# Start of a fused attention, rational and PReLU kernel: two load queues, shared key blocks, a wide exponential, more idle products, paired chunks

## The chip, the cores and the metric

The kernel runs on one core of a Trainium2 chip. The metric is device time in microseconds (us), the median of several runs. The engines are TensorE (PE; its weight loads are PEld), VectorE (DVE), ScalarE (ACT), GpSimd (POOL, unused here) and SyncE (SP), which issues the transfers.

## The reference

Attention over 4 batches, 8 heads, 576 positions, head width 64, each query seeing 32 keys; then two MLPs over 2304 tokens (512 to 2048 to 512):

```python
mask_plain = (rel >= 0) & (rel < window)                                             # heads 0-3
mask_dil = (rel >= 0) & (rel < window * dilation) & (rel % dilation == 0)            # heads 4-7
attn = softmax(where(mask, scale * q @ k.T, -1e9)); x = attn @ v
h = x @ w_in;  P = a0 + a1*h + a2*h**2 + a3*h**3;  Q = 1 + |b0|*|h| + |b1|*h**2
x = (P / (Q + 1e-6)) @ w_out                    # first MLP
h = x @ w_in2; out = (max(h, 0) + alpha * min(h, 0)) @ w_out2   # second MLP
```

The weights come as 64-bit words.

## The kernel before

The 2304 tokens are cut into five blocks (256, 512, 512, 512, 512). Attention is cut into 18 units of 256 queries and four heads, plain or dilated; block 0 has units 0 (plain) and 1 (dilated), block 1 units 2 to 5, and so on. A unit is eight cells: 32 queries against 64 keys, for four heads on four groups of partitions. Its steps:

- `qk_load`, `v_load` (L430, L442): transfers by SP. Each cell brings its 64 keys, so the 32 keys that two neighbouring cells share come twice.
- `att_s` (L456): on PE, the mask is added into two PSUM banks by products of an identity with a mask (L471, bf16), then 32 score products (L482, f32; the trace counts two matmuls and two weight loads for each).
- `att_max`, `att_exp` (L491, L502): DVE takes each row's maximum; ACT computes eight exponentials, 64 columns each, with the maximum as bias and the sum as by-product (L513).
- `att_den`, `att_norm`/`att_norm2`, `att_t` (L518 to L541): one over the sum, the scaling (on DVE for units 0 and 1, on ACT later, L528), the transpose on DVE.
- `att_pv` (L543): products with the values (L557); `att_hi`, `att_lo` (L587): copies into the x tiles.

A first-MLP step takes a chunk of 128 hidden features: `inproj` (L613) multiplies the block's x by a chunk of `w_in` into a bank `ps_h` (two buffers); `rat_1`, `rat_2` (L640, L648) compute the rational function on ACT and DVE; `outproj1` (L668) adds the chunk's share of the output into four banks `ps_y`. Chunks go in pairs J. Block 0 runs in plain f32, one product where later blocks take three. `w_convert` (L383) turns a pair of raw 64-bit chunks into f32: two passes on ACT (L395), three on DVE (L398, L400). `w_split` (L409) makes the two parts for blocks 1 to 4. The second MLP works on the stored result of the first.

A planner, `in_order_of_need` (L155), fixes the order of PE, DVE, ACT and SP up to its own 197 us (`ORDERED`): with costs from `_cost` (L122) it takes, on the engine that can start first, the ready instruction with the longest path behind it. Idle products (bf16, 128x512, of a zeroed tile `warm`) come last: PE gets them where nothing else is ready in the plan. There are 8 at the start (`WARM`, L961) and 20 more (`FILLS`, L965). The order of the first loads is a string: c the mask table, a a unit's queries, keys and values, p the coefficients, w a weight chunk. The planner also models instruction supply on PE: it counts words per product, and a block of 256 may not be opened sooner than 6.5 us after the last.

```python
ORDER = "capawwwwawwwwwwwwww"
words = 4 if todo[k].ins[0].dtype == F32 else 2
if (fetched + words) // FETCH > fetched // FETCH:
    start = max(start, opened + FETCH_NS)
```

Of the kernel before, what the change touches and what calls it, by code (L numbers as in the profile page):

```python
# [31 lines left out]
FILLS = (20,)  # L32
W_BIAS = 2.0 ** -112
# [13 lines left out]
KW = UB // 2 * HEADS * CELL  # L47
# [5 lines left out]
ORDER = "capawwwwawwwwwwwwww"  # L53


class Unit:


    def __init__(self, block, dilated, part):
# [6 lines left out]
        self.vw = self.segs * (self.nb + 1) * D  # L66

# [82 lines left out]

def _is_filler(i):
    return i.engine == mybir.EngineType.PE and i.ins[0].dtype == BF16 and _columns(i.outs[0]) == FILL


def in_order_of_need(tc, nc, places, late):  # L155
# [18 lines left out]
    for k, i in enumerate(todo):  # L174
# [7 lines left out]
        if i.engine == Engine.SP:  # L182
            size[k] = writes[0][2] - writes[0][1], (writes[0][4] - writes[0][3])
# [48 lines left out]
    for k in reversed(range(n)):  # L232
        own = costs[k][1] if todo[k].engine != Engine.SP else 2500 + size[k][0] * size[k][1] / 400
# [9 lines left out]
    free = {Engine.PE: 1300.0, Engine.DVE: 800.0, Engine.Activation: 1500.0, Engine.SP: 730.0}  # L243
# [6 lines left out]
    fetched, opened = 63, 0.0  # L250
    for _ in range(n):
        pick = None
        for e, w in waiting.items():
            if not w:
# [6 lines left out]
        k = max((k for k in waiting[e] if ready_at[k] <= limit), key=lambda k: level[k])  # L261
# [12 lines left out]
        if e == Engine.SP:  # L274
# [22 lines left out]
def attn_rational_prelu_kernel(  # L297
# [9 lines left out]
    alpha: bass.AP,  # L307
# [18 lines left out]

    def bank(tag, bufs=1):
# [10 lines left out]
    co = cp.tile([128, 6], F32, name="co")  # L338
# [4 lines left out]
    alp = cp.tile([128, NC], F32, name="alp")  # L343
# [112 lines left out]
    def att_s(U, tags=("aS", "aP"), banks=None):  # L456
# [3 lines left out]
        kinds = [[UNITS[U].mask(2 * jj + p) for jj in range(HALF)] for p in range(2)]  # L460
# [30 lines left out]
    def att_max(U):  # L491
        a = att[U]
        mx = sp.tile([128, 8], F32, tag="mx", name="mx", bufs=2)
        nm = a["nm"] = sp.tile([128, 8], F32, tag="nm", name="nm", bufs=2)
        for p in range(2):
# [107 lines left out]
    h_t, tmp, g_t, acc = {}, {}, {}, {}  # L603

# [8 lines left out]
    def inproj(item):  # L613
# [3 lines left out]
        hp = bank("h", 2)[:, :BLOCKS[n]]  # L617
# [335 lines left out]

    nc.scalar.preload_act_table_set("natural_log_exp_and_others")
# [244 lines left out]
```

## Time and profile before

| | us |
|---|---|
| median of three runs | 866.67 (866.16 to 866.96) |
| profiled execution | 867.52 |
| its span, first to last instruction | 865.7 |
| PE busy | 843.1 (97%) |
| DVE busy | 722.8 (83%) |
| ACT busy | 560.2 (65%) |

The span is that of the profiled execution; the other 1.8 us of it lie outside. A busy PE counts products at either clock, so the granted clock has to be read beside it.

### The profile page before, as it was taken

To read this page: it belongs to the slowest core of one execution; us is meant where nothing else is said; L and a number is where in the kernel's file an instruction comes from. 1 tells how busy PE (TensorE), PEld (TensorE's weight loads), DVE (VectorE), ACT (ScalarE), POOL (GpSimd) and SP (SyncE) were. 2 spreads that over 40 slices of the span, in tenths; PEclk is the share of its full clock that TensorE was granted. 3 is DMA by queue.
4 is the path that set the end of the run, shared out by engine and by line. 5 is a ranking of instruction groups with operands and counts; after the bars stand their busy time and mean duration, and the time that the engine had idled before them with its cause. 6 is when DMAs were issued, how large, how long until landed. Compare 5 with 4: busy or idle time off the path is not lost.

```text
span 865.7 us, 15595 instructions
## 1 busy us (share of the span) xinstructions
PE 843.1 (97%) x6258; PEld 717.7 (83%) x6260; DVE 722.8 (83%) x1066; ACT 560.2 (65%) x1092; POOL 0.2 (0%) x4
## 2 busy tenths in 40 slices
PE   7888999999999989999999999999999999999998
PEld 4677878888888777788888898988989899899896
DVE  4799999989889878899899899999976769767652
ACT  4799986777866786665757566557553546635424
POOL 0000000000000000000000000000000000000000
PEclk8899999999999999999999999999999999999999
DMA  9892211133632355320202333315120102300001
GB/s 354 307 405 79 81 50 36 53 101 135 236 104 103 120 181 187 108 88 15 76 25 83 125 122 121 98 61 175 70 80 24 49 30 75 122 26 25 0 1 73
DMA packets 33912, 90.93 MB, mean 105 GB/s; under 512 B 4016, under 2 KB 11568, under 8 KB 33840
## 3 DMA queue, kind: packets, MB, share of 16 engines
q1 hardware_dynamic: 33840, 89.94, 29.6%
q8 instruction: 49, 0.80, 0.4%
q14 instruction: 23, 0.19, 0.1%
HBM read 74.72 MB, written 15.20 MB: 104 GB/s over the span
## 4 chain that ended last, share of the span: by engine, by line
PE 74%; DVE 11%; ACT 11%; issue 2%; DMA 1%; SPq 0%; ACTq 0%
PE ps_h L838 20%; PE ps_y L696 15%; PE ps_h L624 14%; PE ps_y L676 13%; PE ps_aS L696 4%; PE ps_aP L696 4%; ACT p L513 3%; ACT p L528 2%; DVE tc L656 2%; DVE tb L652 1%; DVE tc L646 1%; ACT ta L643 1%; DVE tc L657 1%; DVE tc L645 1%; ACT tc L644 1%
## 5 line engine op out<-in xcount | busy, mean ns | idle before, releaser
L624 PE MATMUL ps_h<-xh,winh 128*128 128x512 f32 x256 | 102.8, 401 | 3.9 <-DVE tc L646 3.8
L624 PE MATMUL ps_h<-xl,winh 128*128 128x512 f32 x256 | 100.6, 393 | 1.1 <-DVE xl L594 1.1
L624 PE MATMUL ps_h<-xh,winl 128*128 128x512 f32 x256 | 100.3, 392 | 0.0
L676 PE MATMUL ps_y<-gh,wouth 128*128 128x512 f32 x256 | 99.2, 390 | 0.6 <-ACT gh L665 0.6
L676 PE MATMUL ps_y<-gl,wouth 128*128 128x512 f32 x256 | 99.7, 389 | 0.0
L676 PE MATMUL ps_y<-gh,woutl 128*128 128x512 f32 x256 | 99.7, 389 | 0.0
L643 ACT ACTIVATE ta<-ps_h,root 128x512 f32<-128x512 f32 (+1 forms) x80 | 52.7, 659 | 51.1 <-DVE tc L656 32.4
L696 PE MATMUL ps_y<-wouth,gl 128*128 128x512 f32 x192 | 75.0, 391 | 0.0
L696 PE MATMUL ps_y<-woutl,gh 128*128 128x512 f32 x192 | 74.9, 390 | 0.0
L696 PE MATMUL ps_y<-wouth,gh 128*128 128x512 f32 x192 | 74.3, 390 | 0.0
L843 ACT ACTIVATE n<-h 128x768 f32<-128x768 f32 x48 | 40.5, 843 | 42.8 <-DVE h L868 23.3
L624 PEld LDWEIGHTS ps_h<-xh,winh 128*128 128x128 f32 x256 | 48.4, 189 | 17.2 <-DVE tc L646 6.1
L645 DVE TENSOR_TENSOR tc<-tc,ps_h 128x512 f32<-128x512 f32 (+1 forms) x80 | 50.1, 627 | 12.8 <-ACT tc L644 12.7
L845 DVE SCALAR_TENSOR_TENSOR n<-n,alp,h 128x768 f32<-128x768 f32 x48 | 48.8, 1016 | 13.7 <-ACT h L844 13.0
L644 ACT ACTIVATE tc<-ps_h,co 128x512 f32<-128x512 f32 (+1 forms) x80 | 60.1, 751 | 0.0
L624 PEld LDWEIGHTS ps_h<-xl,winh 128*128 128x128 f32 x256 | 48.5, 190 | 11.3 <-DVE xl L594 1.8
L676 PEld LDWEIGHTS ps_y<-gh,wouth 128*128 128x128 f32 x256 | 48.1, 188 | 10.8 <-ACT gh L665 1.0
L624 PEld LDWEIGHTS ps_h<-xh,winl 128*128 128x128 f32 x256 | 48.4, 189 | 10.3
L734 ACT ACTIVATE st_a<-w 128x1024 fp32r<-128x1024 f32 x24 | 25.4, 1057 | 48.3 <-PE ps_h L838 45.2
L653 ACT ACTIVATE ta<-tb,c1t 128x1024 f32<-128x1024 f32 (+1 forms) x40 | 43.2, 1080 | 20.5 <-DVE tb L652 20.4
L676 PEld LDWEIGHTS ps_y<-gh,woutl 128*128 128x128 f32 x256 | 48.0, 188 | 9.9
L676 PEld LDWEIGHTS ps_y<-gl,wouth 128*128 128x128 f32 x256 | 48.0, 188 | 9.9
(187 smaller groups left out, 2168.9 us busy)
## 6 DMA issues: line engine op xcount, KB each, us to landing
ld_qk<-in_qk_dram SPq DMA_DIRECT2D x16, 768.0 KB, 5.3
w<-w_dram_in SPq DMA_DIRECT2D x24, 512.0 KB, 3.2
raw<-in_w_in_dram SPq DMA_DIRECT2D x16, 512.0 KB, 4.9
raw_inh<-in_w_out_dram SPq DMA_DIRECT2D x13, 512.0 KB, 7.3
out_dram<-os SPq DMA_DIRECT2D x18, 256.0 KB, 2.1
raw_inh<-in_w_in_dram SPq DMA_DIRECT2D x8, 512.0 KB, 8.5
raw_outh<-in_w_in_dram SPq DMA_DIRECT2D x8, 512.0 KB, 9.2
raw_outh<-in_w_out_dram SPq DMA_DIRECT2D x8, 512.0 KB, 9.3
```

The costliest lines, as they stand in the source:

```text
L513: nc.scalar.activation(out=a["p"][:, j * CELL:(j + 1) * CELL], in_=a["s"][p][:, jj * CELL:(jj + 1) * CELL], func=AF.Exp, scale=scale, bias ...
L624: product = nc.tensor.matmul(out=hp, lhsT=w, rhs=x, start=(k == 0), stop=(k == len(pairs) - 1))
L643: nc.scalar.activation(out=ta, in_=hp, func=AF.Abs, scale=root)
L644: nc.scalar.activation(out=tc_, in_=hp, func=AF.Identity, scale=co[:, 3:4], bias=co[:, 2:3])
L645: nc.vector.tensor_tensor(out=tc_, in0=tc_, in1=hp, op=ALU.mult)
L653: nc.scalar.activation(out=ta, in_=tb, func=AF.Ln, bias=c1t)
L676: nc.tensor.matmul(out=yt, lhsT=w[:, m * 128:(m + 1) * 128], rhs=g, start=(c == 0 and i == 0), stop=(c == NC - 1 and i == len(pairs) - 1),)
L696: nc.tensor.matmul(out=yt, lhsT=g[:, tok], rhs=w, start=(first and i == 0), stop=(last and i == 2))
L734: nc.scalar.activation(out=hi, in_=t, func=AF.Copy)
L838: nc.tensor.matmul(out=hp, lhsT=u[:, ws], rhs=x[:, xs], start=(k == 0), stop=(k == 5))
L843: nc.scalar.activation(out=neg, in_=h, func=AF.Relu, scale=-1.0)
L845: nc.vector.scalar_tensor_tensor(out=neg, in0=neg, scalar=alp[:, c:c + 1], in1=h, op0=ALU.mult, op1=ALU.subtract, reverse1=True)
```

## The change

- **Loads.** The mask table goes over ACT's queue. SP begins with unit 0's queries and keys, as one transfer into the single `ld_qk` buffer, then unit 1's, then unit 0's values and two weight chunks. `coef` and `alpha` are one transfer.
- **Keys.** A run of neighbouring cells shares its keys: 5 blocks of 32 keys for four cells in a row, 6 for two rows of two, in place of 8 (`run`, `kb`, `kw`, `block_of`). The first four cells go to one bank, the last four to the other, where it was even and odd.
- **Unit 0's exponential.** DVE adds the negated maximum to the scores (two passes, 256 columns each), ACT takes one exponential of 512 columns, DVE sums (one pass).
- **Idle products.** 40 in place of 20 after the first 8, in groups of two; the second of a group, and all mask products of a unit but the first, are written with `ldweights=False` (`held`). The planner keeps a group together and counts one word for such a product.
- **Block 0's pairs.** The two chunks of a pair lie in one bank, and `rat_1` works on both at once, 512 columns.
- The planner treats ACT's transfer as a transfer (`_is_dma`).

```diff
-KW = UB // 2 * HEADS * CELL
+KW = 6 * HEADS * QB
-ORDER = "capawwwwawwwwwwwwww"
+ORDER = "kkvwwvpwwkvwwwwwwwwww"
@@ class Unit
+        self.run = min(self.nb, UB // 2)
+        self.kb = UB // 2 // self.run * (self.run + 1)
+        self.kw = self.kb * HEADS * QB
+    def block_of(self, jj):
+        return jj // self.run * (self.run + 1) + jj % self.run
@@ in_order_of_need
+        if e == Engine.PE and held is not None:
+            k = held
+        else:
+            k = max((k for k in waiting[e] if ready_at[k] <= limit and not _holds(todo[k])), key=lambda k: level[k])
...
-            words = 4 if todo[k].ins[0].dtype == F32 else 2
+            words = 4 if todo[k].ins[0].dtype == F32 else 1 if _holds(todo[k]) else 2
@@ attn_rational_prelu_kernel
+    def held(out, lhsT, rhs, start, stop):
...
+        pe.add_instruction(mybir.InstMatmult(
...
+            start_tensor_calc=start, stop_tensor_calc=stop, tile_size=(128, 128), tile_position=(0, 0), ldweights=False,
@@ qk_load
-        if U < 2:
+        w = QW + UNITS[U].kw
+        if U == 1:
...
-            t = ldp.tile([128, QW + KW], F32, tag="qk", name="ld_qk", bufs=1)
-            nc.sync.dma_start(out=t, in_=qk[U])
+            t = ldp.tile([128, 4 * BLK], F32, tag="qk", name="ld_qk", bufs=1)
+            nc.sync.dma_start(out=t[:, :w], in_=qk[U][:, :w])
@@ att_s
-                nc.tensor.matmul(
+                (held if p or j0 else nc.tensor.matmul)(
...
+                    key = (i * sh.kb + sh.block_of(jj)) * QB
...
-                        rhs=a["k"][rows(p), at * CELL:(at + 1) * CELL],
+                        rhs=a["k"][rows(p), key:key + CELL],
@@ att_exp
+        if U == 0:
...
+                nc.vector.tensor_tensor(
...
+            nc.scalar.activation(out=a["p"], in_=a["p"], func=AF.Exp, scale=scale)
+            nc.vector.tensor_reduce(out=sm[:, :UB], in_=cells, axis=AX.X, op=ALU.add)
@@ inproj
+            if c % 2 == 0:
+                h_pair[c // 2] = bank("h", 2)
+            hp = half(h_pair[c // 2], c % 2, BLOCKS[n])
@@ rat_1
+        if J < NC // 2:
+            if i == 0:
+                return
+            hp = h_pair.pop(J)
+            ta, tb, tc_ = (t[:, :2 * block_of(J)] for t in tmp[J])
@@ body
+    nc.scalar.dma_start(out=msk, in_=consts)
...
-        for _ in range(k):
-            nc.tensor.matmul(out=t[:, :FILL], lhsT=warm[:, :128], rhs=warm, start=True, stop=True)
+        for i in range(k * GROUP):
+            (held if i % GROUP else nc.tensor.matmul)(
```

**What the order becomes.** Line numbers move by 29 to 69 (L624 becomes L684, L676 L744, L557 L611, L482 L523, L395 L433); L359 is the line of `held`. First SP's queue from its first transfer, before:

```order
L975 DMA msk<-in_consts_dram 128x384
L434 DMA ld_in<-in_qk_dram 128x512
L435 DMA ld_out<-in_qk_dram 128x1024
L449 DMA ld_v<-in_vals_dram 128x576
L977 DMA co<-in_coef_dram 128x6
L978 DMA alp<-in_alpha_dram 128x16
```

and of the change:

```order
L478 DMA ld_qk<-in_qk_dram 128x1152
L473 DMA ld_in<-in_qk_dram 128x512
L474 DMA ld_out<-in_qk_dram 128x768
L488 DMA ld_v<-in_vals_dram 128x576
L407 DMA raw_inh_131<-in_w_in_dram 128x1024
L407 DMA raw_outh_133<-in_w_in_dram 128x1024
L488 DMA ld_v<-in_vals_dram 128x768
```

Unit 0's queries and keys are first, unit 1's come ahead of all values, and the first two weight chunks ahead of unit 1's values; the mask table is gone from this queue.

On DVE, from unit 0's first maximum (banks 191 and 192 are unit 0's, 243 and 244 unit 1's), before:

```order
L496 TENSOR_REDUCE mx<-ps_y_191 128x4
L496 TENSOR_REDUCE mx<-ps_y_192 128x4
L984 TENSOR_SCALAR ba<-ba 128x1
L500 TENSOR_SCALAR nm<-mx 128x8
L496 TENSOR_REDUCE mx<-ps_y_243 128x4
L496 TENSOR_REDUCE mx<-ps_y_244 128x4
```

and of the change (207 and 208 unit 0's, 254 and 255 unit 1's):

```order
L538 TENSOR_REDUCE mx<-ps_y_207 128x4
L538 TENSOR_REDUCE mx<-ps_y_208 128x4
L557 TENSOR_TENSOR p<-ps_y_207,mx 128x256
L557 TENSOR_TENSOR p<-ps_y_208,mx 128x256
L538 TENSOR_REDUCE mx<-ps_y_254 128x4
L538 TENSOR_REDUCE mx<-ps_y_255 128x4
L562 TENSOR_REDUCE sm<-p 128x8
L543 TENSOR_SCALAR nm<-mx 128x8
```

Unit 1's scaled maximum (`nm`), for which its exponentials wait, stands behind unit 0's two additions and its sum.

On PE, from the last product of chunk 1 (unit 2's 32 score products lie where lines are left out), before:

```order
L624 MATMUL ps_h<-xh_404,win_308 128x256 x2
L482 MATMUL ps_aS<-ld_qk 32x64
...
L624 MATMUL ps_h<-xh_357,win_314 128x256 x2
L624 MATMUL ps_h<-xh_404,win_314 128x256 x2
...
L676 MATMUL ps_y_735<-gl,wout_360 128x256
```

and of the change:

```order
L684 MATMUL ps_h<-xh_421,win_325 128x256 x2
L523 MATMUL ps_aS<-ld_qk 32x64
...
L1034 LDWEIGHTS warm
L1034 MATMUL ps_h<-warm 128x512
L359 LDWEIGHTS warm
L359 MATMUL ps_h<-warm 128x512
...
L684 MATMUL ps_h<-xh_374,win_331 128x256 x2
...
L611 MATMUL ps_aS<-pts,ld_v 64x32 x2
```

Twelve idle products stand between unit 2's scores and chunk 2; 4 stand before unit 1's scores, 16 behind them and 8 between the value products of units 0 and 1 (before: 10, 7 and none, and 3 ahead of unit 0's scores). Every product of `held` has a weight load of its own in front. Chunks 2, 3, 4 and half of 5, then unit 2's value products and unit 3's scores, now come ahead of the first output products; before, only chunks 2 and 3 and six of the matmuls of chunk 4's did.

## Rows read from the trace of the kernel before

**Rows 1.** Windows by stage: PE, PEld, DVE, ACT, POOL busy, PE clock, DMA share, GB/s.
```profile
17.40:26.00 8.60, 8.60 (x144) 7.11 (x144) 3.93 (x8) 3.41 (x8) 0.00 (x0) 0.61 1.03 408
17.50:18.00 0.50, 0.50 (x24) 0.50 (x27) 0.50 (x2) 0.07 (x1) 0.00 (x0) 0.50 0.99 391
24.50:25.00 0.50, 0.50 (x4) 0.39 (x3) 0.44 (x1) 0.03 (x1) 0.00 (x0) 1.00 0.98 393
26.00:36.00 10.00, 6.79 (x38) 5.21 (x26) 9.79 (x21) 9.94 (x36) 0.00 (x0) 0.92 1.02 408
36.00:42.00 6.00, 6.00 (x153) 4.84 (x153) 3.66 (x9) 3.96 (x8) 0.00 (x0) 0.85 0.35 97
42.00:60.00 18.00, 15.43 (x203) 12.77 (x203) 17.27 (x39) 18.00 (x68) 0.00 (x0) 1.00 1.01 393
60.00:80.00 20.00, 19.35 (x230) 16.57 (x229) 19.36 (x39) 20.00 (x56) 0.00 (x0) 1.00 0.45 165
```
**Rows 2.** Timeline of PE: start, length, instruction, count, idle before and releaser.
```profile
1.48 1.89 PE L961 MATMUL ps_h<-warm 128*128 128x512 bf16 x4 [1.48 <-DVE warm L957]
...
7.34 0.86 PE L482 MATMUL ps_y<-ld_out,ld_in 64*32 64x64 f32 x64
8.36 2.11 PE L965 MATMUL ps_h<-warm 128*128 128x512 bf16 x9 [0.16 <-issue]
...
14.12 1.36 PE L557 MATMUL ps_y<-p,ld_v 32*64 32x64 f32 x64 [1.25 <-ACT p L513]
17.35 1.93 PE L557 MATMUL ps_y<-p,ld_v 32*64 32x64 f32 x64 [1.87 <-ACT win L395]
19.22 6.13 PE L624 MATMUL ps_h<-xh,win 128*128 128x256 f32 x16
...
33.26 2.68 PE L676 MATMUL ps_y<-gl,wout 128*128 128x256 f32 x8 [3.21 <-DVE rd L522]
...
38.13 0.24 PE L557 MATMUL ps_aS<-pts,ld_v 32*64 32x32 f32 x2
...
42.69 1.89 PE L676 MATMUL ps_y<-gl,wout 128*128 128x256 f32 x8
...
48.00 1.56 PE L624 MATMUL ps_h<-xh,win 128*128 128x256 f32 x6 [1.69 <-DVE tc L646]
```
**Rows 3.** Mask table: PE's weight loads, shortest/median/longest ns, first and last start.
```profile
L471 PEld LDWEIGHTS <-msk x7: 130/147/147, 2.7 to 4.0; 128*128 128x128 bf16 x7
```
**Rows 4.** Timeline of SP's queue, its first issue; landing of keys of units 0, 1.
```profile
0.73 0.39 SPq L975 DMA_DIRECT2D msk<-in_consts_dram  x1
...
DMA to landing us min/median/max: 4.3/4.7/5.1
```
**Rows 5.** Timeline of DVE.
```profile
8.22 0.76 DVE L496 TENSOR_REDUCE mx<-ps_y 128x4 f32<-128x256 f32 x2 [6.80 <-PE ps_y L482]
...
35.37 0.71 DVE L541 STREAM_TRANSPOSE pts<-p 128x512 f32<-128x512 f32 x1 [0.21 <-ACT p L528]
```
**Rows 6.** Timeline of ACT.
```profile
14.37 0.35 ACT L513 ACTIVATE p<-ps_y,nm 128x64 f32<-128x64 f32 x1
...
23.04 0.47 ACT L643 ACTIVATE ta<-ps_h,root 128x256 f32<-128x256 f32 x1 [2.60 <-PE ps_h L624]
...
27.94 0.63 ACT L654 ACTIVATE ta<-ta 128x512 f32<-128x512 f32 x1
...
33.32 2.02 ACT L528 ACTIVATE p<-p,rd 128x64 f32<-128x64 f32 x8
```
**Rows 7.** Windows from the start to two stops of PE for "issue"; columns as above.
```profile
0.00:55.30 55.30, 45.05 (x728) 32.73 (x730) 37.04 (x87) 39.94 (x142) 0.20 (x4) 0.91 0.91 347
0.00:84.50 84.50, 72.45 (x1110) 55.97 (x1112) 65.60 (x145) 68.91 (x220) 0.20 (x4) 0.94 0.76 290
```
**Rows 8.** Timeline of PE at these stops.
```profile
55.75 0.48 PE L676 MATMUL ps_y<-gl,wout 128*128 128x256 f32 x1 [0.87 <-issue]
...
85.82 0.24 PE L482 MATMUL ps_aP<-ld_qk 64*32 64x64 f32 x1 [1.67 <-issue]
```

More of the change, by code (lines that the diff above doesn't have):

```diff
@@ L232, in in_order_of_need @@
     for k in reversed(range(n)):
-        own = costs[k][1] if todo[k].engine != Engine.SP else 2500 + size[k][0] * size[k][1] / 400
+        own = costs[k][1] if not _is_dma(todo[k]) else 2500 + size[k][0] * size[k][1] / 400
         step = costs[k][0]
@@ L250, in in_order_of_need @@
     fetched, opened = 63, 0.0
+    pes = [k for k in range(n) if todo[k].engine == Engine.PE]
+    holder_of = {a: b for a, b in zip(pes, pes[1:]) if _holds(todo[b])}
+    held = None
     for _ in range(n):
@@ L253, in in_order_of_need @@
         for e, w in waiting.items():
+            w = [k for k in w if k == held or not (held is not None and e == Engine.PE or _holds(todo[k]))]
             if not w:
@@ L260, in in_order_of_need @@
         limit = max(t, free[e]) + SLACK
-        k = max((k for k in waiting[e] if ready_at[k] <= limit), key=lambda k: level[k])
+        if e == Engine.PE and held is not None:
+            k = held
+        else:
+            k = max((k for k in waiting[e] if ready_at[k] <= limit and not _holds(todo[k])), key=lambda k: level[k])
+        if e == Engine.PE:
+            held = holder_of.get(k)
         waiting[e].remove(k)
@@ L459, in att_s @@
         s = a["s"] = banks or [bank(tag) for tag in tags]
-        kinds = [[UNITS[U].mask(2 * jj + p) for jj in range(HALF)] for p in range(2)]
+        sh = UNITS[U]
+        kinds = [[sh.mask(p * HALF + jj) for jj in range(HALF)] for p in range(2)]
         def rows(p):
@@ L499, in att_max @@
             )
-        nc.vector.tensor_scalar_mul(out=nm[:, :UB], in0=mx[:, :UB], scalar1=scale)
+        if not (U == 0):
+            nc.vector.tensor_scalar_mul(out=nm[:, :UB], in0=mx[:, :UB], scalar1=scale)
     def att_exp(U):
@@ L616, in inproj @@
             assert all(U in done for U in range(NEED[n])), "early"
-        hp = bank("h", 2)[:, :BLOCKS[n]]
+        if n:
+            hp = bank("h", 2)[:, :BLOCKS[n]]
+        else:
+            if c % 2 == 0:
+                h_pair[c // 2] = bank("h", 2)
+            hp = half(h_pair[c // 2], c % 2, BLOCKS[n])
         pairs = [
@@ L624, in inproj @@
             product = nc.tensor.matmul(out=hp, lhsT=w, rhs=x, start=(k == 0), stop=(k == len(pairs) - 1))
+            if n == 0 and c % 2 and k == 0:
+                late.append((product.ins.name, h_last[c - 1]))
         h_t[item] = hp
+        h_last[c] = product.ins.name
         return product.ins.name
@@ L959, in attn_rational_prelu_kernel @@
     idle = bank("h", 2)
-    for _ in range(WARM):
-        nc.tensor.matmul(out=idle, lhsT=warm[:, :128], rhs=warm, start=True, stop=True)
+    for k in range(WARM):
+        (held if k % 2 else nc.tensor.matmul)(out=idle, lhsT=warm[:, :128], rhs=warm, start=True, stop=True)
     def fill(t, k):
-        for _ in range(k):
-            nc.tensor.matmul(out=t[:, :FILL], lhsT=warm[:, :128], rhs=warm, start=True, stop=True)
+        for i in range(k * GROUP):
+            (held if i % GROUP else nc.tensor.matmul)(
+                out=t[:, :FILL], lhsT=warm[:, :128], rhs=warm, start=True, stop=True
+            )
     for U, what in enumerate(ORDER):
-        if what == "a":
-            U = ORDER[:U].count("a")
-            qk_load(U)
-            v_load(U)
+        if what in "kv":
+            (qk_load if what == "k" else v_load)(ORDER[:U].count(what))
         elif what == "w":
             w_loads(1, 1)
-        elif what == "c":
-            nc.sync.dma_start(out=msk, in_=consts)
-        else:
-            nc.sync.dma_start(out=co, in_=coef)
-            nc.sync.dma_start(out=alp, in_=alpha)
+        else:
+            nc.sync.dma_start(out=cf, in_=coef)
     nc.vector.memset(c1t, C1)
@@ L1156, in _pack_attention @@
             for bb in range(sh.nb):
[L1157 removed]
+                p, jj = divmod(g * sh.nb + bb, UB // 2)
                 t = t0 + bb * QB
+                k0 = sh.block_of(jj)
                 qa[p, :, jj] = qs[:, t:t + QB].transpose(2, 0, 1)
[L1160 removed]
+                for n in range(2):
+                    ka[p, :, :, k0 + n] = ks[:, t + n * QB:t + (n + 1) * QB].transpose(2, 0, 1)
             for b in range(sh.nb + 1):
```

52 lines of the change are left out of this document (35 added, 17 removed).

## The prediction

> **What bounds the kernel now.** I read the windows by stage first, then PE's timeline, then those of DVE, ACT and SP over the first 50 us, because PE is 97% busy over the span and can only be helped where it is not. In the windows [rows 1] the reader is to see where that is: PE is busy throughout from 17.4 to 26 us but at a mean clock of 0.61, from 26 to 36 us it is idle for 3.21 us, and from 42 to 60 us for 2.57 us. ACT is then busy all of the time (18.00 of 18.00, 20.00 of 20.00) and DVE nearly so. So the first 60 us are bound by the start, then by ACT and DVE, the rest by PE, which keeps any lead that it has been given. PE's timeline [rows 2] shows the start: the value products of units 0 and 1 wait 1.25 and 1.87 us; behind these waits the first sixteen matmuls of chunks 0 and 1 take 6.13 us, where later eight of the same width take 1.89. The granted clock is 0.50 (1.2 GHz, not 2.4) from about 17.5 us, after those two idle stretches, and 1.00 again at 24.5 [rows 1]. ACT waits 2.60 us for chunk 0 [rows 6], and PE later 3.21 us for the first converted output weights [rows 2].
>
> **The change, step by step**, on the profiled execution (867.52 us; its clock of events is used below, and the median, 866.67, is 0.85 lower).
>
> *Unit 0's scores.* The three idle products ahead of them go; at the early pitch that is 4 in 1.89 us less the tail, 0.43 each, so 1.28 us [rows 2]. But unit 1's two mask products become eight narrow ones, each with its load of 0.147 us [rows 3]: 8 x 0.147 less 0.43 is 0.75 more. From 7.34 us to 6.8 to 6.9. Data do not hold this: keys landed at earliest 4.3 us after their issue [rows 4], and now the unit's single transfer is issued at 0.73 us, the place of the mask table, with 0.59 MB in place of 0.79. The second queue saves one issue, about 0.4 us, and what it hides behind is this PE work: I cost it at nothing. Unit 2's keys now wait for unit 0's scores, since they share a buffer; behind that wait SP has the weight chunks, but the wait ends near 8 us, when 4.1 MB ahead of it still take until about 13 us at 0.4 MB per us (the 408 GB/s of [rows 1]). Nothing.
>
> *Unit 0's softmax.* Scores end at 7.7. Two maxima 0.76 [rows 5], two additions (none in the trace; nothing if something else is late, at most that of another two-operand pass; the nearest row is the same 256 columns out of PSUM, 0.76 for two): 9.2. The wide exponential is ACT's 128x512 pass, 0.63 [rows 6], in place of eight at 0.29: 9.9. DVE meanwhile takes unit 1's maxima (its scores come 4 idle products later, 8.8 to 9.6): 9.7 to 10.4; then the sum over 512 columns, twice 0.34: 11.1; scale, sum and reciprocal 0.4; scaling and transpose 0.6 and 0.7 [rows 5]: 12.8. PE has 16 idle products of 0.215 (9 in 2.11 [rows 2]) from 9.8 and comes to unit 0's value products at 13.3, before 14.12.
>
> *Unit 1.* Its `nm` is ready at 11.2, eight exponentials at 0.29 end at 13.7 (before 14.7 [rows 6]); from there to its value products it took 2.63 us [rows 2, 6], so 16.3. PE: 13.3 + 1.36, then 8 idle products: 16.5. Before 17.35. No idle stretch of PE above 0.2 us is left in front, so I take the clock to stay at 1.00; unit 1's products then take 1.36 us, not 1.93. Chunk 0 starts at 17.9, before 19.22.
>
> *Chunks 0 and 1* take 3.6 us, twice the 1.89 us of eight [rows 2]: end at 21.5, before 25.35. This is the main gain, 3.9 us.
>
> *To unit 2's value products.* Unit 2's scores end at 22.3 (0.86), twelve idle products at 25.0, chunks 2, 3, 4 and half of 5 (3.5 x 1.8) at 31.3. On ACT in the new order, from 21.6: the paired pass and its second (0.57, 0.66), four weight passes (0.57 each), two passes of the pair (0.62, 0.52), eight exponentials (2.36), eight scalings (2.02 [rows 6]): 9.0, so 30.6, and the transpose 0.71 [rows 5]: 31.3. Unit 2's value products start at 31.3, before 38.13. The 3.21 us wait is gone, as these products no longer stand behind it. The late thing next is ACT's chain, level with PE. The twelve idle products cost nothing only because of that chain; without it they are 2.6 us. Value products, masks, unit 3's scores (2.4 us), half a chunk (0.9) and eight output products (3.6): 38.2. The same work was done at 42.69 + 1.89 = 44.58. **-6.4.** From below: if unit 2's chain takes as long behind its scores as before (25.9 to 38.13, 12.2), the lead is 3.6. From above: all that PE lost from 17.4 to 60 us [rows 1], idle 3.21 + 2.57 and by the clock 0.39 x 8.6 + 0.08 x 10 + 0.15 x 6 = 5.1, plus 1.3 at the start, less 2.6 for idle products: 9.6.
>
> *After that.* The wait of 1.69 at 48.00 [rows 2]: chunks 6 and 7 find their bank freed, but unit 3's chain is ACT's again; of it I take **-0.5**. The paired passes also save ACT and DVE work; PE lost only 0.65 us from 60 to 80 us [rows 1], so that is worth 0 to 0.65; I take 0.
>
> *Instruction supply.* Between two stops for "issue" PE carried out (1110 + 1112) - (728 + 730) = 764 instructions [rows 7], three blocks of 256 within the count's error; stops of 0.87 and 1.67 us [rows 8] fall where block ends are close in time. `held` drops no load in the order, so it saves nothing here. Counted on in the new order (four per f32 product), one block ends eleven instructions ahead of unit 3's value products and the next inside unit 4's scores, the pattern of the 1.67 us stop; nowhere else are two so close. New 1.67 (between 0.87 and both stops together, 2.54), old 2.54 gone: **-0.9**. The Trainium skill (Runtime: NRT & Kernel Launch, "Instruction fetch mechanics") says that crossing such a block is mostly hidden. By that rule the new stop costs nothing and the sum would be 1.7 lower; the trace does not agree, it shows the stops.
>
> Sum: -6.4 - 0.5 - 0.9 = **-7.8**; 867.52 becomes 859.7, the median 866.67 about **858.9**.
>
> **Rivals.**
> 1. *The chain of ACT and DVE does not shorten.* For it: both are full from 26 to 36 us (9.94 and 9.79 of 10 [rows 1]) and PE's earlier chunks only queue there. Against: they idled 5.2 and 4.7 us of the 8.6 before that [rows 1]. Lead 3.6, the later terms half: 862.5.
> 2. *No stop at the new block ends*, whatever made the old ones: 858.9 - 1.7 = 857.2. Beside it stands the page's rule above. For it: other ends of blocks pass without a stop. Against: both stops are 764 instructions apart.
> 3. *Slower: the clock falls anyway.* Block ends lie at unit 1's first score and three quarters through unit 0's value products, about 5.5 us apart; a stop there in front of 8 idle products, as in [rows 8], can bring the clock to 0.50 as the waits at 12.8 and 15.5 did. Then it costs the stop 1.7, chunks 0 and 1 3.4, the twelve idle products 2.5 (0.43 in place of 0.215) and chunks 2 and 3 3.4: 11, which moves unit 2's value products from 31.3 to about 42, against 38.13: 870.5. It decides only if the clock stays down for over 14 us; before it was down from 17.5 to about 24.5.
> 4. *It does not do what it says.* The loads of `held` show that one part does not; if the loads too change nothing, 866.7.
>
> **How the numbers follow.** Forecast 0.62, rival 1 0.22, rival 2 0.10, rival 3 0.04, rival 4 0.02. The measurement can tell about 0.2% (1.7 us) from no change: faster 0.94, same 0.02, slower 0.04. The range goes from the upper bound of the lead with the stops' gain (866.67 - 9.6 - 0.9 - 0.65 = 855.5) to just past rival 1, 863.5; outside lie rivals 3 and 4 and what is left of the others, under 2 in 10.
>
> **What would show it.** Right: a granted clock of 1.00 from 17 to 26 us; chunks 0 and 1 in 3.6 us, done near 21.5; unit 0's value products near 13.3, unit 2's near 31.3; no wait of 3 us of the first output products, which end near 38; one stop for issue in unit 4's scores. Wrong: a clock of 0.50 after 17 us, unit 2's value products after 34 us, a lead at 44 us that is gone at 120 us, or new stops for issue.

## The result, and the profile after

The changed kernel takes 859.89 us (median of four runs, 857.41 to 860.48); the kernel before took 866.82 in the same comparison. The ratio is 0.9913, 95% interval 0.9902 to 0.9925: faster by about 7.5 us, well beyond 0.2%. The forecast was 858.9, the range 855.5 to 863.5. The profiled execution took 859.46, 8.06 less than the one of before (867.52).

| after, profiled execution | us |
|---|---|
| span | 857.7 |
| PE busy | 841.9 (98%) |
| DVE busy | 721.2 (84%) |
| ACT busy | 555.7 (65%) |

The windows by stage, answering to [rows 1] (PE, PEld, DVE, ACT, POOL busy, PE clock, DMA share, GB/s):

```profile
17.40:26.00 8.60, 8.39 (x158) 5.85 (x158) 7.47 (x20) 6.26 (x14) 0.00 (x0) 1.00 1.03 409
26.00:36.00 10.00, 9.71 (x174) 7.86 (x173) 9.37 (x18) 9.89 (x35) 0.00 (x0) 1.00 0.93 361
36.00:42.00 6.00, 6.00 (x29) 5.30 (x28) 5.91 (x14) 6.00 (x27) 0.00 (x0) 1.00 0.94 341
42.00:60.00 18.00, 18.00 (x353) 15.52 (x352) 17.49 (x34) 18.00 (x53) 0.00 (x0) 1.00 1.02 403
60.00:80.00 20.00, 19.39 (x225) 16.74 (x224) 19.66 (x37) 19.64 (x48) 0.00 (x0) 1.00 0.26 81
```

From 17.4 to 60 us PE is idle for 0.50 us in all, where it was 5.78, and the granted clock is 1.00 (2.4 GHz) throughout, where it was 0.61, 0.92 and 0.85 up to 42 us. PE's timeline, answering to [rows 2] and [rows 8]:

```profile
5.10 0.23 PE L511 MATMUL ps_y<-msk 128*128 128x64 bf16 x1 [1.73 <-DMA msk<-in_consts_dram]
...
8.19 1.19 PE L523 MATMUL ps_y<-ld_qk 64*32 64x64 f32 x64
9.71 0.63 PE L359 MATMUL ps_h<-warm 128*128 128x512 bf16 x1 [0.34 <-issue]
10.14 0.63 PE L1034 MATMUL ps_h<-warm 128*128 128x512 bf16 x1
...
11.96 0.38 PE L359 MATMUL ps_h<-warm 128*128 128x512 bf16 x1 [0.16 <-issue]
12.17 0.38 PE L1034 MATMUL ps_h<-warm 128*128 128x512 bf16 x1
...
15.29 1.13 PE L611 MATMUL ps_y<-p,ld_v 32*64 32x64 f32 x64
...
18.31 1.13 PE L611 MATMUL ps_y<-p,ld_v 32*64 32x64 f32 x64
19.37 3.72 PE L684 MATMUL ps_h<-xh,win 128*128 128x256 f32 x16
...
26.79 6.28 PE L684 MATMUL ps_h<-xh,win 128*128 128x256 f32 x28 [0.21 <-DVE tc L714]
33.15 0.24 PE L611 MATMUL ps_aS<-pts,ld_v 32*64 32x32 f32 x2
...
36.41 3.62 PE L744 MATMUL ps_y<-gl,wout 128*128 128x256 f32 x16
...
73.38 0.30 PE L611 MATMUL ps_aS<-pts,ld_v 32*64 32x32 f32 x4 [0.61 <-issue]
118.16 0.30 PE L611 MATMUL ps_aS<-pts,ld_v 32*64 32x32 f32 x4 [1.18 <-issue]
```

The reader is to see a new wait of 1.73 us for the mask table and, behind it, work at half pace: unit 0's scores take 1.19 us where they took 0.86, idle products follow one another at 0.43 us up to 10.57 and at 0.21 to 0.22 from 11.96 on. For 512 columns these paces match the two levels of the clock, 1.2 and 2.4 GHz (512 / 1.2 = 427 ns, 512 / 2.4 = 213 ns). The trace's record of the granted clock begins only at 10.68 us here, at 1.00, and at 7.05 in the kernel before; a window that reads 1.00 ahead of that has no record behind it. Unit 0's scores start at 8.19, 0.85 later than before. From there it gets better: chunks 0 and 1 take 3.72 in place of 6.13, unit 2's value products start at 33.15 in place of 38.13, ahead of the first sixteen output matmuls (36.41). The waits of 3.21, 1.69, 0.87 and 1.67 of before have no counterpart. The two above 0.5 us that are left with "issue" stand in front of products that need a transposed tile, and DVE's transposes end at 72.58 + 0.70 = 73.28 and 117.35 + 0.71 = 118.06, 0.1 us before PE starts: they are waits for DVE.

### The profile page after: what moved, and what is told of

Read it like the earlier page. It is cut to its first block, busy times and chain, and to the rows that moved or that the text cites. A ratio compares the mean times of both kernels' runs of the same rounds, so it can differ in the third digit from the quotient of the medians.

```text
span 857.7 us, 15588 instructions
## 1 busy us (share of the span) xinstructions
PE 841.9 (98%) x6272; PEld 716.5 (84%) x6276; DVE 721.2 (84%) x1052; ACT 555.7 (65%) x1061; POOL 0.2 (0%) x4
## 4 chain that ended last, share of the span: by engine, by line
PE 76%; DVE 11%; ACT 8%; DMA 3%; issue 3%; SPq 0%; ACTq 0%; DVEq 0%
PE ps_h L906 20%; PE ps_y L744 15%; PE ps_y L764 15%; PE ps_h L684 14%; PE ps_aP L764 4%; PE ps_aS L764 4%; ACT p L567 2%; DVE tc L724 1%; DMA raw<-in_w_in_dram 1%; ACT p L582 1%; DVE tc L714 1%; DVE tc L713 1%; DVE tc L725 1%; PE ps_aS L611 1%; DVE tb L720 1%
## 5 line engine op out<-in xcount | busy, mean ns | idle before, releaser
L684 PE MATMUL ps_h<-xh,winh 128*128 128x512 f32 x256 | 102.6, 401 | 4.9 <-DVE tc L714 4.2
L684 PE MATMUL ps_h<-xl,winh 128*128 128x512 f32 x256 | 100.7, 393 | 0.9 <-DVE xl L648 0.9
L684 PE MATMUL ps_h<-xh,winl 128*128 128x512 f32 x256 | 100.3, 392 | 0.0
L744 PE MATMUL ps_y<-gl,wouth 128*128 128x512 f32 x256 | 99.8, 390 | 0.0
L744 PE MATMUL ps_y<-gh,woutl 128*128 128x512 f32 x256 | 99.7, 389 | 0.0
L744 PE MATMUL ps_y<-gh,wouth 128*128 128x512 f32 x256 | 99.2, 390 | 0.1
L711 ACT ACTIVATE ta<-ps_h,root 128x512 f32<-128x512 f32 x72 | 50.1, 696 | 46.8 <-DVE tc L724 34.0
L684 PEld LDWEIGHTS ps_h<-xh,winh 128*128 128x128 f32 x256 | 48.4, 189 | 18.6 <-DVE tc L714 6.2
L913 DVE SCALAR_TENSOR_TENSOR n<-n,cf,h 128x768 f32<-128x768 f32 x48 | 48.8, 1017 | 13.2 <-ACT h L912 12.6
L684 PEld LDWEIGHTS ps_h<-xl,winh 128*128 128x128 f32 x256 | 48.5, 189 | 11.0 <-DVE xl L648 1.5
L684 PEld LDWEIGHTS ps_h<-xh,winl 128*128 128x128 f32 x256 | 48.5, 189 | 10.2
L712 ACT ACTIVATE tc<-ps_h,cf 128x512 f32<-128x512 f32 x72 | 56.7, 788 | 0.0
L744 PEld LDWEIGHTS ps_y<-gh,wouth 128*128 128x128 f32 x256 | 48.0, 188 | 10.3 <-ACT gh L733 0.5
L744 PEld LDWEIGHTS ps_y<-gh,woutl 128*128 128x128 f32 x256 | 48.1, 188 | 10.0
L744 PEld LDWEIGHTS ps_y<-gl,wouth 128*128 128x128 f32 x256 | 48.0, 188 | 10.0 <-DVE gl L734 0.2
L713 DVE TENSOR_TENSOR tc<-tc,ps_h 128x512 f32<-128x512 f32 x72 | 48.9, 679 | 7.2 <-ACT tc L712 7.1
```

Source lines behind the costliest of these rows:

```text
L712: nc.scalar.activation(out=tc_, in_=hp, func=AF.Identity, scale=co[:, 3:4], bias=co[:, 2:3])
L713: nc.vector.tensor_tensor(out=tc_, in0=tc_, in1=hp, op=ALU.mult)
L744: nc.tensor.matmul(out=yt, lhsT=w[:, m * 128:(m + 1) * 128], rhs=g, start=(c == 0 and i == 0), stop=(c == NC - 1 and i == len(pairs) - 1),)
L913: nc.vector.scalar_tensor_tensor(out=neg, in0=neg, scalar=alp[:, c:c + 1], in1=h, op0=ALU.mult, op1=ALU.subtract, reverse1=True)
```

## The experiments

All times are medians of 4 to 12 runs against the kernel before on the same chip. "Stop" is an idle time of PE for "issue" within unit 4's scores; "packet" is the start of the transfer of 16 KB of PE's instructions that comes next before it (one record of queue q8 in the trace); "clock" is that of 42 to 60 us. The last four columns are those of one execution, the profiled one, and it need not be like the median: e5's took 861.48, where four of its other five took 857.5 to 858.7, and e3's took 871.71.

| run | us | ratio to before | unit 3's value products at | packet at | stop | clock |
|---|---|---|---|---|---|---|
| changed kernel | 859.89 | 0.9913 (0.9902 to 0.9925) | 44.71 | 42.86 | none | 1.00 |
| e1 mask table first | 860.77 | 0.9932 (0.9920 to 0.9943) | 41.64 | 44.94 | 3.55 | 0.91 |
| e2 20 idle products | 866.53 | 0.9999 (0.9990 to 1.0007) | 45.84 | 49.38 | 3.76 | 0.91 |
| e3 before, 40 idle | 868.69 | 1.0030 (1.0013 to 1.0046) | 50.21 | 53.74 | 3.68 | 0.86 |
| e4 no pairs in a bank | 868.03 | 1.0018 (1.0007 to 1.0030) | 47.25 | 50.37 | 3.24 | 0.91 |
| e5 e1, two products ahead | 858.61 | 0.9913 (0.9896 to 0.9929) | 43.26 | 45.43 | 2.41 | 0.91 |
| e6 one product back | 858.52 | 0.9903 (0.9890 to 0.9916) | 43.74 | 41.81 | none | 1.00 |
| e7 no `held` | 865.13 | 0.9981 (0.9972 to 0.9991) | 45.06 | 47.95 | 3.21 | 0.91 |
| e8 no wide exponential | 860.46 | 0.9931 (0.9919 to 0.9944) | 44.46 | 41.60 | none | 1.00 |
| e9 e1, weights spread | 858.54 | 0.9907 (0.9893 to 0.9921) | 42.37 | 42.88 | 0.90 | 1.00 |
| e10 weights spread | 858.94 | 0.9914 (0.9899 to 0.9929) | 44.19 | 41.46 | none | 1.00 |
| e11 extra copies | 863.34 | 0.9960 (0.9948 to 0.9973) | 44.30 | 47.44 | 3.48 | 0.91 |
| e12 e2, weights spread | 860.85 | 0.9925 (0.9911 to 0.9938) | 45.05 | 46.40 | 1.49 | 1.00 |

**e1_mask_first.**

```diff
-    nc.scalar.dma_start(out=msk, in_=consts)
+    nc.sync.dma_start(out=msk, in_=consts)
```

The planner's start time for ACT goes back with it to that of the kernel before.

> The mask table is again the first transfer of SP's queue; all else of the change is kept. Theory (the wait of 1.73 us for the mask table, and the half rate that follows it, move everything behind them): the table lands some 1.9 us after its issue as it did before, the mask products begin at 3.2 to 3.5 us in place of 5.10, unit 0's scores near 6.5 to 7.0 in place of 8.19, unit 2's value products near 31.5 in place of 33.15, and the time falls by 1.2 to 2.0 us against the changed kernel. Rival (the chain of ACT and DVE, full from 26 us on, or unit 0's keys, now issued 0.44 us later, swallow it): unit 2's value products stay within 0.5 us of 33.15 and the time within 0.5 us of the changed kernel's.

PE's timeline and a window of e1:

```profile
3.16 0.26 PE L511 MATMUL ps_y<-msk 128*128 128x64 bf16 x1
...
5.11 0.86 PE L523 MATMUL ps_y<-ld_qk 64*32 64x64 f32 x64
...
13.39 0.42 PE L611 MATMUL ps_y<-p,ld_v 32*64 32x64 f32 x11 [0.71 <-issue]
...
15.13 1.13 PE L611 MATMUL ps_y<-p,ld_v 32*64 32x64 f32 x64
16.20 3.72 PE L684 MATMUL ps_h<-xh,win 128*128 128x256 f32 x16
...
47.41 0.21 PE L523 MATMUL ps_aP<-ld_qk 64*32 64x64 f32 x1 [3.55 <-issue]
```

```profile
42.00:60.00 18.00, 14.45 (x239) 12.19 (x234) 13.63 (x28) 14.20 (x43) 0.00 (x0) 0.91 0.91 345
```

At its place the theory holds and more: the table lands 2.0 us after its issue, the scores start 3.08 us sooner and at full pace, chunk 0 at 16.20 in place of 19.37. The clock's record begins at 4.46 us, at 1.00. But the time does not fall: PE stops for 3.55 us within unit 4's scores, and from 49 to 52 us the granted clock is 0.50 (1.2 GHz). Neither expectation had this. What it is was the next question, since the prediction had put a stop at this place and the changed kernel showed none.

**e2, e3, e4** undo or isolate one part each.

```diff
-GROUP = 2
+GROUP = 1
```


> Twenty idle products after the first eight, as before, in place of forty; all else of the change is kept, and the planner orders anew. Theory (the idle products keep the clock up, which is the largest single gain): PE stands idle for more than 1 us ahead of the value products of units 0 or 1, the granted clock reads 0.50 after some 17 to 18 us, chunks 0 and 1 take about 6 us in place of 3.72, and 3 to 4.5 us of the gain of 7.5 are given back. Rival 1 (what counts is only that unit 2's value products come ahead of the first output products): the clock falls and the time moves by less than 1 us, as PE waits for ACT afterwards in any case. Rival 2 (all of the gain hangs on it): 6 us or more are given back.

```diff
-FILLS = (20,)
+FILLS = (40,)
```


> The kernel before with forty idle products in place of twenty, and nothing else. Theory (clock): granted clock 1.00 from 17 to 26 us, chunks 0 and 1 in 3.7 us in place of 6.13, and 3 to 4.5 us less than the kernel before. Rival (the order of unit 2's value products and the first output products, and the wait of 3.21 us for the converted weights, hold the rest): the clock stays up and the time falls by less than 1 us, since the wait of 3.21 grows by what the chunks gain.

```diff
-        if n:
-            hp = bank("h", 2)[:, :BLOCKS[n]]
-        else:
...
+        hp = bank("h", 2)[:, :BLOCKS[n]]
```


> Block 0's two chunks of a pair lie in two banks again, with two passes of 256 columns for each step of the rational function; all else is kept. Theory (PE is the bound after 36 us and has hardly any idle time, so the passes saved on ACT and DVE are worth 0 to 0.65 us): within 0.7 us of the changed kernel. Rival (the chain of ACT that unit 2's value products wait for has eight passes of this kind in it, at 0.1 to 0.2 us saved each, and that chain is what ends last from 26 to 33 us): 1 to 2.5 us slower than the changed kernel, unit 2's value products at 34 to 35.5 us.

The first window of e2, then that of e3:

```profile
17.40:26.00 8.60, 8.60 (x151) 7.12 (x152) 5.79 (x16) 4.55 (x10) 0.00 (x0) 0.80 1.03 409
```
```profile
17.40:26.00 8.60, 8.45 (x90) 6.32 (x92) 5.68 (x10) 4.62 (x10) 0.00 (x0) 0.80 1.03 409
```

PE's timeline of e2, of e3 and of e4, in this order:

```profile
17.39 1.13 PE L611 MATMUL ps_y<-p,ld_v 32*64 32x64 f32 x64 [2.04 <-ACT win L433]
18.45 5.41 PE L684 MATMUL ps_h<-xh,win 128*128 128x256 f32 x16
...
51.89 0.24 PE L523 MATMUL ps_aP<-ld_qk 64*32 64x64 f32 x1 [3.76 <-issue]
...
112.83 0.50 PE L744 MATMUL ps_y<-gh,wouth 128*128 128x512 f32 x1 [3.05 <-ACT gh L733]
```

```profile
35.60 2.08 PE L676 MATMUL ps_y<-gl,wout 128*128 128x256 f32 x4 [3.05 <-DVE gl L657]
...
56.23 0.31 PE L482 MATMUL ps_aS<-ld_qk 64*32 64x64 f32 x1 [3.68 <-issue]
```

```profile
33.74 1.13 PE L732 MATMUL ps_y<-gl,wout 128*128 128x256 f32 x4 [3.05 <-DVE gl L713]
...
52.80 0.26 PE L523 MATMUL ps_aS<-ld_qk 64*32 64x64 f32 x1 [3.24 <-issue]
```

e2 and e4 each give back all of the gain, e3 gains nothing, so each result is worse than the theory that was put to it: by the verdict alone the whole gain would hang on the idle products and again on the pairs. The traces tell it apart. Up to unit 3's value products e2 is 1.14 us later than the changed kernel and e4 2.55; the rest comes behind, with a stop of 3.2 to 3.8 us and a lower clock after it, at the same place in all of them. At unit 4's value products e2 is 4.66 us later (60.93 against 56.27) and at unit 6's 4.34; then PE waits 3.05 us for ACT at 112.83, the clock reads 0.50 from 114.2 to 117.6 us, and at unit 7's it is 7.52 later. So some 3 of e2's 6.6 us go there and not at the stop, and no run tells why. e3 does not test what it was made for: in spite of its forty idle products unit 1's value products wait 2.10 us and the clock from 17.4 to 26 us is 0.80, not 1.00. In e3 and e4 the first output products stand ahead of unit 2's value products again and wait 3.05 us, as in [rows 2].

**Where the stop comes from.** The windows from the start to the stop count PE's matmuls and loads, called records below; of e1, e2, e4, in this order:

```profile
0.00:45.00 45.00, 40.44 (x726) 29.53 (x731) 33.84 (x74) 34.73 (x109) 0.20 (x4) 1.00 0.98 382
```
```profile
0.00:50.00 50.00, 41.48 (x727) 31.11 (x730) 34.54 (x75) 35.67 (x110) 0.20 (x4) 0.97 0.92 356
```
```profile
0.00:51.00 51.00, 41.63 (x727) 28.77 (x732) 36.17 (x82) 36.52 (x115) 0.20 (x4) 0.97 0.91 351
```

1457, 1457 and 1459 records; the stop of 0.87 of before came at 728 + 730 = 1458 [rows 7, 8]. So PE stops after the same number of instructions, whatever they are; in all traces with such a stop it is record 1457 to 1461 (the expectation of e5, below, has 1469). In the changed kernel PE passes this count at 46.6 us without a stop. The DMA rows of the two kernels, queue q8, over 41 to 44.5 us in e1 (no such row), 44.5 to 47 in e1, and 42.5 to 44.5 in the changed kernel:

```profile
q1 hardware_dynamic: 393, 1.43, 102.7%
```
```profile
q1 hardware_dynamic: 278, 0.99, 99.0%
q8 instruction: 1, 0.02, 2.8%
```
```profile
q1 hardware_dynamic: 224, 0.80, 99.6%
q8 instruction: 1, 0.02, 3.1%
```

The columns are packets, MB and share. The stops of one trace lie about a multiple of 256 records apart (1458 and 2222 in [rows 7], 699 and 1461 in e9), with one packet of 16 KB to each 256, so a packet is taken to be 256 instructions, and the end of a block is found by counting. In e1 it starts at 44.94, when PE has already run out (43.86), takes 1.11, and PE goes on 1.36 after its end; in the changed kernel it starts at 42.86, before PE has begun the value products of unit 3 and the scores of unit 4, which with the masks are 284 records in 2.2 us (44.71 to 46.86). The data transfers fill the DMA engines at either packet (99.0 and 99.6%): what differs is when it comes. In all ten traces with a stop at this count, those of the table and that of the kernel before, PE goes on 1.3 to 1.6 us after the packet's end.

**e5 and e6** move one or two output products across unit 3's value products and unit 4's scores, nothing else.

```diff
+    move = 2
...
+        pe[first:last + move] = pe[last:last + move] + pe[first:last]
```


> As e1_mask_first, and two output products (L744 in the changed kernel) that stood behind unit 3's scores now stand ahead of unit 3's value products; nothing else in PE's order changes. Counted in the order (four records per f32 product, matmuls and loads), unit 3's value products then begin at record 1230 in place of 1222; in the changed kernel they begin at 1226, and the stops of e1 to e4 all lie at record 1469 or so of the trace. Theory (instruction supply: a fetch of 256 records starts only when PE's queue has gone past the end of a block; in e1 that end lay so close ahead of the value products that PE's wait for their transposed input held the fetch up, by some 4 us): the stop of 3.5 us in unit 4's scores is gone, the clock stays at 1.00 from 42 to 60 us, an instruction packet is fetched before unit 3's value products begin and not 3 us after, and the time is 2 to 4 us below e1's 860.8, near 857. Rival (the stop has to do with the transfers that are under way when PE is that early, not with where the block ends): the stop stays within 0.5 us of 3.5 and the time within 0.7 us of e1's.

```diff
+    move = -1
...
+        pe[first + move:last] = pe[first:last] + pe[first + move:first]
```


> The changed kernel with one output product fewer ahead of unit 3's value products (it stands behind unit 4's scores instead): they begin at record 1222 in place of 1226, as in e1; nothing else in PE's order changes. Theory (instruction supply, as in e5): a stop of 3 to 4 us appears in unit 4's scores near record 1469, the granted clock falls behind it, and the time is 2.5 to 4.5 us above the changed kernel's 859.9. Rival (one product of 0.45 us moved cannot matter): within 0.5 us of the changed kernel.

The window of e6 and the stop of e5:

```profile
42.00:60.00 18.00, 18.00 (x353) 15.55 (x352) 17.42 (x33) 18.00 (x51) 0.00 (x0) 1.00 1.01 398
```
```profile
47.87 0.26 PE L533 MATMUL ps_aP<-ld_qk 64*32 64x64 f32 x1 [2.41 <-issue]
```

This theory falls. e6 has the record numbers of e1 and no stop; its time is within the changed kernel's interval. e5 has a better distance than either and, in its profiled execution, a stop of 2.41; its median is 2.2 us below e1's, as the theory expected, but that can't be put down to a stop that is gone, as four other executions that took some 3 us less have no trace. It is not the distance between the block's end and the wait that decides.

**e7 and e8.**

```diff
-        pe.add_instruction(mybir.InstMatmult(
...
+        return nc.tensor.matmul(out=out, lhsT=lhsT, rhs=rhs, start=start, stop=stop)
```


> Every product that was written with ldweights=False is an ordinary one; the planner then counts two words for it, and groups are no longer kept together. The program has the same loads either way. Its order differs a little: 18 idle products ahead of chunk 2 in place of 12, 3 in place of 8 between the value products of units 0 and 1, and unit 3's value products begin at record 1218. Theory (instruction supply): a stop of 3 to 4 us in unit 4's scores and 2.5 to 5 us more than the changed kernel, although nothing that is computed or waited for differs. Rival (the flag itself saves nothing and the order differs little): within 0.7 us of the changed kernel.

```diff
-        if U == 0:
-            cells = a["p"].rearrange("p (t k) -> p t k", k=CELL)
...
```


> Unit 0's softmax again with eight exponentials of 64 columns (DVE's two additions and its sum go); all else of the change is kept, and the planner puts 24 idle products ahead of unit 0's value products. They begin 0.7 to 1.3 us later than the changed kernel's 15.29 by the row sums (eight exponentials of 0.29 against two additions of 0.74, one exponential of 0.63 and a sum of 0.68 of which the sum and part of the rest lie beside other work). Unit 3's value products begin at record 1233, behind the end of a block by more than in the changed kernel, so the theory of instruction supply expects no stop in unit 4's scores and 0.3 to 1.5 us more than the changed kernel. Rival (any other order brings a stop, the changed kernel just has luck): a stop of 3 us or more and 2.5 us or more slower.

Both came out as expected in the stop (3.21 and none), e8 in time too; e7's 5.2 us are just above the 2.5 to 5 expected. The reason given for e7 has fallen with e6, but the point stays: a flag that drops no load changes the planner's counts and with them the order, and without it 5.2 us go. The wide exponential is worth 0.6 us by the medians and 1.5 by the ratios, which these runs can't tell from nothing; in its trace e8 is level with the changed kernel up to unit 6's value products (0.15 us later).

**e9, e10, e11** change the data transfers alone; PE's order is to the last product that of e1, of the changed kernel and of the changed kernel.

```diff
-            w_loads(1, 4)
+            w_loads(1, 4 if J < 1 else 2 if J < 3 else 6)
```
e9 has e1's edit besides; this line alone is e10.

> As e1_mask_first, with the weight transfers spread otherwise: four of the eight that SP issued between unit 3's keys and unit 4's values (32.9 to 39.2 us in e1) come behind unit 5's keys; PE's order is that of e1 to the last product. Theory (the packet of 256 instructions that unit 4's scores need waits behind data: in e1 the transfers ran at 376 to 422 GB/s in every us from 28 to 47, and the packet came at 44.94): with about 2.1 MB less ahead of it the transfers pause near 40 to 43 us, the packet comes before 43 us, the stop of 3.5 us and the half clock after it are gone, unit 2's value products stay near 30 to 31 us, and the time is 855.5 to 858.0 against e1's 860.8. Rival (the packet's time does not hang on the data transfers): a stop of 2.5 us or more stays and the time lies within 0.7 us of e1's; a second rival, that the weights then come too late, would show as a wait of ACT or DVE for a raw chunk after 48 us.

> The changed kernel with the weight transfers spread as in e9; PE's order is that of the changed kernel. Theory: its profiled execution had no stop in unit 4's scores, but its executions differ by 3 us (857.4 to 860.5), as they would if the packet came in time in some and late in others; with the pause all are like the best one, 857 to 858.5, and they differ by less than 2 us. Rival: no difference, 859 to 861 with the same spread.

```diff
+            for i in range(3 if J == 0 else 0):
+                extra = dp.tile([128, 2 * DM], U32, name=f"extra{i}")
+                nc.sync.dma_start(out=extra, in_=w1_in[i].bitcast(U32))
```


> The changed kernel with three copies of 0.5 MB of weights to a place in memory that nobody reads, issued by SP ahead of unit 3's values, so that the pause of the transfers from 34 to 38 us (172 to 226 GB/s in the changed kernel) is filled; PE's order is unchanged. Theory (the packet waits behind data): the packet that came at 34.69 in 0.8 us now takes 3 us or more, the next one comes after unit 3's value products have begun, a stop of 2 to 4 us appears in unit 4's scores, the clock falls behind it, and the time is 2 to 5 us above the changed kernel's 859.9. Rival (the packets do not care, and ACT and DVE have their data early): within 0.7 us.

Windows and the stop of e9, then of e11:

```profile
42.00:60.00 18.00, 17.10 (x349) 14.61 (x348) 15.96 (x32) 16.58 (x47) 0.00 (x0) 1.00 0.82 308
```
```profile
45.49 0.21 PE L523 MATMUL ps_aP<-ld_qk 64*32 64x64 f32 x1 [0.90 <-issue]
```
```profile
26.00:36.00 10.00, 10.00 (x176) 8.37 (x175) 9.31 (x19) 9.89 (x33) 0.00 (x0) 1.00 1.09 438
42.00:60.00 18.00, 14.53 (x191) 12.28 (x191) 13.46 (x27) 12.40 (x41) 0.00 (x0) 0.91 1.00 374
```
```profile
49.98 0.26 PE L523 MATMUL ps_aS<-ld_qk 64*32 64x64 f32 x1 [3.48 <-issue]
```

These two show that the data traffic is a cause of the stop. e11 adds only copies that nobody reads: the packet that took 0.8 us from the block's end (33.90 to 34.69 in the changed kernel) takes 3.5 (33.45 to 36.91), the next one comes at 47.44, PE stops for 3.48, the clock falls, and 3.45 us are lost (4.1 by the ratios). e9 takes 2 MB out of the way: the packet comes 2 us sooner than in e1, the stop shrinks from 3.55 to 0.90 where it was expected to go, the clock stays, and 2.2 us come back (the time is 0.5 above the range expected). e10 lies between its two expectations (858.94, its runs 1.7 us apart) and can't be told from the changed kernel.

**e12_idle20_paced** is e2 with the spread of e9.

> As e2_idle20 (twenty idle products), with the weight transfers spread as in e9; PE's order is that of e2. In e2 unit 3's value products began at 45.84 us, only 1.14 later than in the changed kernel, and the stop of 3.76 us and the half clock behind it came after them. Theory (what e2 gave back was for the most part that stop, and the forty idle products themselves are worth 1 to 2 us): the stop falls below 1.5 us, the clock from 42 to 60 us is 1.00, the clock from 17 to 26 us is still near 0.80, and the time is 860.0 to 862.5, against e2's 866.5. Rival (the clock from 17 us on is itself worth 3 us or more, as the prediction had it): with the stop gone the time still is 863 to 865. Second rival (the transfers do not matter here): the stop of more than 3 us stays, 866 to 867.

```profile
17.40:26.00 8.60, 7.72 (x154) 6.62 (x155) 7.48 (x20) 6.10 (x13) 0.00 (x0) 1.00 1.03 409
...
42.00:60.00 18.00, 15.03 (x326) 12.70 (x327) 15.93 (x31) 15.87 (x50) 0.00 (x0) 1.00 0.76 284
```
```profile
48.83 0.24 PE L523 MATMUL ps_aP<-ld_qk 64*32 64x64 f32 x1 [1.49 <-issue]
...
107.77 0.50 PE L744 MATMUL ps_y<-gh,wouth 128*128 128x512 f32 x1 [1.36 <-ACT gh L733]
```

With 20 idle products and the transfers spread it takes 860.85, 5.7 us less than e2. So with the transfers spread the second twenty idle products are worth 860.85 - 858.94 = 1.9 us (e12 against e10; 1.0 by the ratios), not the 6.6 of e2. What they give by themselves is not isolated even so: e12 still has a stop of 1.49, and a wait of 1.36 for ACT at 107.77 behind which the clock falls to 0.50, and e10 has neither. One expectation failed: the clock from 17 to 26 us is 1.00 here and 0.80 in e2, though the idle products are the same; unit 1's value products waited 1.72 us here, 2.04 in e2, 1.87 before.

## Why the prediction was right, step by step

The sum was right, and the case it was made for happened, but several terms were off and cancelled: that the number came out so near is luck. The lead is 4.55 us where the sum had 6.4, and grows by 3.1 and 0.4 behind it where the sum had 0.5 and 0.9: 8.0 in all.

- **Unit 0's scores**: this step failed. "The second queue saves one issue [...] I cost it at nothing": the table landed 4.3 us after its issue where it had taken 1.9, beside 0.59 MB of keys issued in the same instant, and PE waited 1.73. The clock's record begins later with it: at 8.07 to 10.68 us in the nine traces with the table on ACT's queue, at 4.46 to 7.33 in the five with the table first on SP's. The Trainium skill (DMA: Bandwidth & Descriptors, "Issuing engines are not separate DMA queues") says that transfers interleave on the same engines whoever issues them; the trace agrees (4.3 us beside the keys, 2.0 alone and first in e1), and it speaks against this part of the change. Scores at 8.19, not 6.8 to 6.9; value products at 15.29 and 18.31, not 13.3 and 16.5.
- **The clock and chunks 0 and 1**: right, 1.00 and 3.72 (3.6). Its worth was over-sized: "the main gain, 3.9 us", where e2, with a clock of 0.80 there, is only 1.14 us late at unit 3's value products (there chunks 0 and 1 took 5.41, not 6.13).
- **Unit 2's value products**: the path was right, the start not. From chunk 0 they took 33.15 - 19.37 = 13.8 us, forecast 31.3 - 17.9 = 13.4. The sixteen matmuls end at 36.41 + 3.62 = 40.03 in place of 38.2, so the lead is 44.58 - 40.03 = 4.55, not 6.4. The term was 1.85 too large, 1.5 of it from the start of chunk 0 (19.37, not 17.9). The paired bank, costed at 0 beyond its shorter passes in this chain, is worth 2.55 us by unit 3's value products, in the order that e4 has without it.
- **The 1.69 us wait**: "of it I take -0.5" was too little. By unit 4's value products, with the same 80 chunk matmuls and 48 output matmuls done before, the lead is 63.93 - 56.27 = 7.66: 3.1 more, of which 0.87 is the first stop.
- **Instruction supply**: the place was right and the event wrong; the term of -0.9 took a new stop of 1.67 off the 2.54 of the old ones, and no new one came. The stop forecast in unit 4's scores did not come in the changed kernel, but in nine of the twelve experiments, at 0.90 to 3.76 us, outside "between 0.87 and both stops together". What was missing is that the packet competes with the data. The rule of the Trainium skill that was weighed there (Runtime: NRT & Kernel Launch, "Instruction fetch mechanics": mostly hidden) holds in the changed kernel and not in e11, whose instructions are the same.
- **After 60 us**: costed at 0. The lead is 113.45 - 104.53 = 8.9 at block 0's first stored output, where the second stop of before has gone too, and 8.0 at the end; the wait of 1.18 for a transpose at 118 takes most of the difference.

Of the rivals, 1 (chain of ACT and DVE) did not happen, 2 (no stop) happened, though not at its 857.2, 3 (a stop and then half clock) happened in e1 to e5, e7 and e11 and cost 2.2 us (e1 against e9; the 5.7 of e2 against e12 have the wait for ACT in them), at unit 4's scores and not where the rival put it; there, in unit 0's value products, e1 has a stop of 0.71 and the clock stays at 1.00. Even then e1, e5, e7 and e11 stay ahead of before.

What stays open: when PE's queue asks for a packet can't be seen in the trace, so it is not explained why e6 and e1, with the same records, get it 1.9 us before and 3.3 us after unit 3's value products begin; e9 and e11 show only that data traffic is one cause. What each part of the change is worth by itself stays open too, as undoing one (e2, e4) brings the stop. Whether spreading the weights would speed up the kernel before was not tried. No version beats the changed kernel by more than the intervals: e6, e9 and e5 at 858.5 to 858.6 lie within them.

## What to carry to other kernels

When undoing each part of a change gives back all of its gain, look for one event that any change of order sets off, and compare the traces at that place before adding up parts. Where a stretch of small instructions follows saturated transfers, try to hold some of the transfers back: here the instructions came over the same engines (e9 gave 2.2 us, e10 nothing, as it had no stop). Look at more than one place for the loss, as with e2's wait for ACT at 112.8 us. A small table that the first instruction needs goes alone and first; a second queue does not make it early.

## What was unexpected in the hardware

- After the wait of 1.73 us PE ran at half pace up to 10.6 us (idle products 0.43 us apart, 64 scores in 1.19), the pace of 1.2 GHz; the windows print a clock of 1.00 there only because the trace has no record of it ahead of 10.68 us. In e1, without that wait, the record begins at 4.46 and the 64 scores take 0.86 at 5.11.
- A packet of PE's instructions started 0.8 us after the end of a block in the changed kernel while the data transfers ran at 172 to 226 GB/s, and 3.5 us after it in e11, with the transfers at 450 to 536; the next one came 1.3 us ahead of the block's end in the changed kernel and 3.3 behind it in e1, both with the transfers near 400. PE goes on 1.3 to 1.6 us after its end, and behind the stops of 2.41 to 3.76 us the granted clock fell to 0.50 (1.2 GHz) for a while, behind those of 0.90 and 1.49 it stayed at 1.00. The length of the idle time does not tell it: behind e12's wait of 1.36 at 107.77 us the clock read 0.50 from 109.5 us.
